# Late weight and input loads tied to 23 score rounds instead of 19, in a two-layer attention and feed-forward kernel

## Chip, core and metric

The kernel runs on one core of a Trainium2 chip. The metric is the device time of one execution in microseconds, the median of several; lower is better. The core's engines are TensorE (PE: matmuls), VectorE (DVE), ScalarE (ACT), GpSimd (POOL) and SyncE (SP), which here issues nearly all DMA transfers.

## What is computed

The input x has 2048 tokens of width 640. Two layers are applied, each an attention block and a feed-forward block with residuals, and both layers use the same weights.

```python
for s in range(N):                                    # 4 segments of 512 tokens, 32 heads of 20
    logits = einsum('bhqd,bhkd->bhqk', qs, ks) * scale + mask
    p = softmax(logits)
    a_dot = einsum('bhqk,bhkd->bhqd', p, vs)
    o = g * (phi(qs) @ M) / (phi(qs) @ z + 1e-6) + (1 - g) * a_dot
    M = M + phi(ks)^T vs ;  z = z + sum(phi(ks))      # memory carried to the next segment
x = x + concat(o) @ wo                                # attention, on layernorm(x)
x = x + relu(layernorm(x) @ w1) @ w2                  # feed-forward, 640 -> 1728 -> 640
# ... both once more
```

Here phi(t) is t + 1 for positive t and exp(t) otherwise; all data are bf16.

## The kernel before

**Work.** One segment of 512 tokens goes through these steps, and several segments are in flight at once. Layer norm on DVE and POOL gives xn_tok, which a DMA transpose turns into xnT (L710). PE projects q and k into stg and v into v_aug (`group`, L667 and L670). The q and k of a segment are spilled to a scratch tensor in HBM (L955) and read back into pad with four heads side by side, two groups of four heads, a "pair", at a time (L1002). Scores are small matmuls from pad (L1186), four at once on quarters of the rows of the array. ACT takes exp of them into PT (L1248), POOL cuts the causal triangle (L1260), PE multiplies by v (L1280), a DMA transpose turns the sums (otu) into otk, and DVE divides (L1366 to L1374). The memory M is read with L1066 and updated with L1123. Then follow wo (L1402 adds the residual), the second layer norm, and the feed-forward block: w1 with relu into hT (L1484, L1485) and hR (L1466), and w2 (L1506 adds the residual).

**Rounds.** A pair has five score rounds (`ROUNDS`), each with two ACT exps; the event ("ex", m, u) says that round u of pair m has been issued, with the tickets of its exps. A segment has four pairs, a layer 16, the kernel 32 and so 160 rounds. Pair 4 is the first of the second segment.

**Order.** All instructions are put in order before the kernel runs, by a planner written into the kernel (`Sched`). Each step of the work is a generator that yields operations with costs and the semaphores that they wait for. In a loop the planner takes the operation that can start first by its own clock, a priority breaking ties, and appends it to its engine's list; what runs on the chip is these fixed lists, each in order, with semaphore waits between them. A DMA load by `dma()` is an operation of SP with an issue time, a rate and a latency in that clock. A matmul group can be issued in two forms: "full", one 128x128 weight tile per matmul (L667), or "cols", the same as four matmuls with 32 weight columns each (L670). The planner takes the form which the array is in, and counts a switch between "full", "cols" and the scores' "rows" form. Because ties and near ties decide, a shift of one operation can reorder what comes after it.

**Loads.** `loads()` fetches the first two segments of x and the weights wq, wk and wv at the start. `late_loads()` fetches the rest through SP's queue, piece by piece, each at first held until a given round has been reached: `n2` is the number of pieces without w2, that is four of x (segment 2), five of wo, four of x (segment 3) and ten of w1 (five with the first half of its columns, name w10, five with the second, w11). The w2 pieces follow from round 25 on, two a round, and wait for a buffer that shares w2's memory (`w2w`); the change leaves them alone. The wait of a piece is on the first exp of its round (`w[:1]`), and SP handles its list in order: a piece that waits holds back the spills, fills and transposes behind it.

Of the kernel before, what the change touches and what calls it, by code (L numbers as in the profile page):

```python
# [38 lines left out]
class Prog:  # L39
# [44 lines left out]
    def dma(self, e, fn, sem):  # L84
        self.pos[e] += 1
        self.dcnt[id(sem)] = self.dcnt.get(id(sem), 0) + 16
        tk = (sem, self.dcnt[id(sem)])
        self.ops[e].append(("op", fn, sem, 16))
        self.info[(id(sem), tk[1])] = ("dma%d" % id(sem), tk[1], dict(self.K[e]))
        return tk  # L90
# [332 lines left out]
def bass_interleave_layers__memory_aug_infini_attn__dense_activation_relu__prompt_kernel(  # L423
    nc, A_x, A_wq, A_wk, A_wv, A_wo, A_beta, B_x, B_w1, B_w2, out,
):
    with contextlib.ExitStack() as es:
# [119 lines left out]
        def late_loads():  # L546

            def x_pieces(s):
                def one(t):
                    return lambda e: e.dma_start(x_sb[:, t, :], xs[:, t, :])  # L550
                return [("x%d" % s, 163840, one(4 * s + i)) for i in range(4)]

            def rows(name, w, src, k):
                return (name, 163840, lambda e: e.dma_start(w[:, k, :], src[128 * k:128 * k + 128, :]))

            def half(k, h):
                cs = slice(h * (DFF // 2), (h + 1) * (DFF // 2))
                return ("w1%d" % h, 221184, lambda e: e.dma_start(w1_r[:, k, cs], B_w1[128 * k:128 * k + 128, cs]))

            pieces = x_pieces(2)  # L560
            pieces += [rows("wo", wo_r, A_wo, k) for k in range(FC)]
            pieces += x_pieces(3)
            pieces += [half(k, h) for h in range(2) for k in range(FC)]
            n2 = len(pieces)
            pieces += [rows("w2", w2_r, B_w2, k) for k in range(NFULL)]
            pieces += [("w2", 81920, lambda e, z=z: e.dma_start(
                w2_r[64 * z:64 * z + DREM, NFULL + z, :], B_w2[NFULL * 128:DFF, :])) for z in range(2)]
            z1 = yield Need("z1")
            sems = {}
            left = {}  # L570
            for name, _, _ in pieces:
                left[name] = left.get(name, 0) + 1
            for n, (name, nbytes, fn) in enumerate(pieces):
                if name not in sems:
                    sems[name] = sem_("d_" + name)
                w = yield Need("ex", *divmod(25 + (n - n2) // 2 if n >= n2 else n * 19 // n2, 5))
                if n == n2:
                    v0 = yield Need("v00")
                    q1 = yield Need("q01")
                    w2w = v0 + q1 + early_done  # L580
                tk = yield dma("sp", sems[name], nbytes, fn, w[:1] + (w2w if n >= n2 else []) + z1, issue=400.0, lat=4500.0)
                left[name] -= 1
                if left[name] == 0:
                    S.set(name, tks=[tk])
# [1009 lines left out]
        S.add(7, consts())  # L1594
        S.add(8, loads())
        S.add(8, late_loads())
        S.run()
        P.waits("sp", [S.last])
# [31 lines left out]
```

The softmax here doesn't subtract the row's maximum and nothing guards it: scores larger than these inputs give would overflow.

## Time and profile before

Time: 556.6 us, the median of 3 runs (555.76 to 557.23). The profiled execution has a span of 554.8 us at a granted TensorE clock of 1.0.

| What | Profile |
|---|---|
| first score round, last score round | 18.5 us, 476 us |
| exps of round 18 and of round 22 end | 58.9 us, 75.6 us |
| SP issues the late pieces of x, wo and w1 | 20.9 to 60.8 us |
| first matmul with w1 | 91.7 us |
| SP issues the w2 pieces | 98.4 to 107.8 us |
| DMA: mean rate, bytes | 110 GB/s, 61.3 MB |

How to read it: the page gives for each engine its busy time and, in the chain, how much of the work that ended last lay on it. A PE row of the timeline merges equal matmuls that follow each other: its start, the time to the end of the last one, its count, and in brackets idle time before it with the instruction that ended it. Matmuls overlap, so the cost of one is the distance from its start to the start of the next, not its length. For a DMA the start is that of its issue, and the landing is given apart.

### The profile page before, as it was taken

How to read it: one execution, taken by the hardware profiler on the slowest of the kernel's cores; microseconds unless marked ns; L12 is line 12 of the kernel's file. 1: busy time of each engine (PE TensorE's matmuls, PEld its weight loads, DVE VectorE, ACT ScalarE, POOL GpSimd, SP SyncE). 2: the span in 40 equal slices, each digit the busy share in tenths (PEclk: the TensorE clock that was granted, in tenths of full speed). 3: DMA queues.
4: the chain of work that ended last, by engine and by line, in shares of the span. 5: the costliest groups of instructions: out<-in, count | busy, mean ns of one | idle time of the engine just before them, and what ended most of it. 6: DMA issues, size and time to landing. Idle time of an engine off the chain costs nothing.

```text
span 554.8 us, 18665 instructions
## 1 busy us (share of the span) xinstructions
PE 545.8 (98%) x8130; PEld 309.3 (56%) x8130; DVE 412.2 (74%) x1061; ACT 407.3 (73%) x516; POOL 190.0 (34%) x302
## 2 busy tenths in 40 slices
PE   8999999999999999999999999999999999999997
PEld 7454554455564555646456544665545654666656
DVE  4967989898799888897878898769885787435102
ACT  5699889889877987798788887679987678432140
POOL 5245344333344344343433443135331443201000
DMA  8595989924945148256176521772439412353101
GB/s 272 131 235 156 222 181 224 231 50 70 187 100 89 39 105 180 50 97 98 21 193 131 92 45 38 184 134 39 69 63 213 95 34 34 84 78 63 40 2 51
DMA packets 130291, 61.30 MB, mean 110 GB/s; under 512 B 109090, under 2 KB 120098, under 8 KB 130210
## 3 DMA queue, kind: packets, MB, share of 16 engines
q1 hardware_dynamic: 129648, 59.58, 50.2%
q8 instruction: 64, 1.05, 0.8%
q10 hardware_dynamic: 562, 0.53, 0.3%
q14 instruction: 17, 0.14, 0.1%
HBM read 20.57 MB, written 12.85 MB: 60 GB/s over the span
## 4 chain that ended last, share of the span: by engine, by line
PE 93%; ACT 2%; DVE 2%; DMA 2%; SPq 0%; issue 0%; POOL 0%; ACTq 0%; POOLq 0%
PE ps L667 45%; PE ps L670 26%; PE ps L1186 9%; PE ps L1280 6%; ACT PT L1248 2%; PE ps L1319 1%; PE ps L1066 1%; PE ps L1123 1%; PE ps L644 1%; DMA otk<-otu 1%; PE ps L1460 1%; DMA beta_bc<-in_A_beta_dram 1%; SPq L982 0%; ACT stg L867 0%; PE ps L758 0%
## 5 line engine op out<-in xcount | busy, mean ns | idle before, releaser
L1248 ACT ACTIVATE PT<-ps 128x1024 bf16<-128x1024 f32 x320 | 308.9, 1027 | 65.0 <-PE ps L1186 59.5
L1260 POOL TENSOR_SCALAR_AFFINE_SELECT PT<-PT 128x512 bf16<-128x512 bf16 x256 | 164.2, 659 | 264.4 <-ACT PT L1248 264.3
L667 PE MATMUL ps<-w_r,hT 128*128 128x320 bf16 x510 | 82.4, 300 | 0.0
L1506 DVE TENSOR_TENSOR x_sb<-x_sb,ps 128x320 bf16<-128x320 bf16 (+1 forms) x65 | 31.1, 478 | 58.9 <-PE ps L670 44.2
L670 PE MATMUL ps<-xnT,w_r 128*32 128x512 bf16 x1112 | 65.4, 379 | 0.2 <-issue 0.2
L1186 PE MATMUL ps<-pad 20*128 20x512 bf16 (+3 forms) x1024 | 63.4, 301 | 1.1 <-ACT PT L1248 0.9
L667 PEld LDWEIGHTS ps<-w_r,hT 128*128 128x128 bf16 x510 | 47.6, 98 | 24.6 <-issue 6.8
L667 PE MATMUL ps<-xnT,w_r 128*128 128x512 bf16 x242 | 59.9, 380 | 0.9 <-DVE hT L1484 0.9
L688 DVE BATCH_NORM_STATS2 stats<-x_sb 128x6 f32<-128x320 bf16 x124 | 55.7, 474 | 2.9 <-DMA x_sb<-in_A_x_dram 2.5
L1485 ACT ACTIVATE hT<-ps 128x512 bf16<-128x512 f32 x56 | 33.4, 597 | 22.9 <-PE ps L670 20.7
L670 PE MATMUL ps<-w_r,hT 128*32 128x320 bf16 (+1 forms) x1340 | 49.0, 294 | 0.0
L1186 PEld LDWEIGHTS ps<-pad 20*128 20x128 bf16 x1024 | 17.9, 92 | 52.1 <-ACT PT L1248 27.8
L1402 DVE TENSOR_TENSOR x_sb<-x_sb,ps 128x320 bf16<-128x320 bf16 x64 | 30.0, 479 | 18.2 <-PE ps L667 10.3
L670 PEld LDWEIGHTS ps<-xnT,w_r 128*32 128x32 bf16 x1112 | 29.0, 97 | 25.2 <-issue 0.4
L1280 PE MATMUL ps<-PT,v_aug 128*21 128x128 bf16 (+3 forms) x896 | 40.4, 301 | 0.0
L670 PEld LDWEIGHTS ps<-w_r,hT 128*32 128x32 bf16 x1340 | 34.8, 97 | 9.0
L667 PE MATMUL ps<-wo_r,oT 128*128 128x320 bf16 x242 | 38.9, 300 | 0.0
L1290 DVE CAST otu<-ps 128x512 bf16<-128x512 f32 x48 | 32.7, 682 | 6.9 <-PE ps L1280 6.3
L1484 DVE TENSOR_SCALAR hT<-ps 128x512 bf16<-128x512 f32 x48 | 32.7, 681 | 6.5 <-PE ps L667 4.3
L704 POOL TENSOR_TENSOR rstd<-lnU,mhalf 128x2 f32<-128x2 f32 (+2 forms) x26 | 20.6, 791 | 46.1 <-DVE lnU L700 43.1
L667 PEld LDWEIGHTS ps<-xnT,w_r 128*128 128x128 bf16 x242 | 21.6, 98 | 25.6 <-issue 4.6
L866 DVE CAST stg<-ps 128x512 bf16<-128x512 f32 x45 | 30.6, 684 | 5.8 <-PE ps L667 5.6
(109 smaller groups left out, 736.9 us busy)
## 6 DMA issues: line engine op xcount, KB each, us to landing
pad<-scr SPq DMA_DIRECT2D x124, 80.0 KB
scr<-stg SPq DMA_DIRECT2D x34, 256.0 KB, 3.1
out_dram<-x_sb SPq DMA_DIRECT2D x15, 160.0 KB, 1.8
w_r<-in_B_w_dram SPq DMA_DIRECT2D x10, 216.0 KB, 2.6
w_r<-in_B_w_dram SPq DMA_DIRECT2D x13, 160.0 KB, 2.9
x_sb<-in_A_x_dram SPq DMA_DIRECT2D x10, 160.0 KB, 3.2
scr<-w_r SPq DMA_DIRECT2D x5, 256.0 KB, 3.2
wv_r<-in_A_wv_dram SPq DMA_DIRECT2D x1, 800.0 KB, 8.8
```

What stands on the lines that cost most here:

```text
L667: return e.matmul(view(dst.ap, b), a, b, start=(k == 0), stop=(k == last))
L670: return e.matmul(view(dst.ap[rows], b), part, b, start=(k == 0), stop=(k == last))
L688: tk = yield dve(320, 1, lambda e, c2=c2: e.bn_stats(stats6[:, t % 12, c2, :], x_sb[:, t, c2 * 320:(c2 + 1) * 320]), xt)
L866: te = yield evac(N, 1, lambda e: e.tensor_copy(sg.ap[:, t0:t0 + N], bk.ap[:, 0:N]), lambda e: e.activation(sg.ap[:, t0:t0 + N], bk.ap[:, ...
L1186: fns.append([(lambda e, z=z, j=j, hh=hh, N=N, o=o, sl=sl, q=hh % 2: e.matmul(slot.ap[:, q, o:o + N], sl.ap[32 * hh:32 * hh + DH, z, 0, 12 ...
L1248: tx = yield act(1024, lambda e, dst=dst, src=src: e.activation(dst, src, ACT.Exp, scale=SCALE), sc + pw)
L1260: tm = yield pool(600.0, lambda e, reg=reg: e.affine_select(out=reg, in_=reg, pattern=[[0, 4], [1, 128]], compare_op=ALU.is_ge, fill=0.0, ...
L1280: fns.append((lambda e, OD, j=j, hh=hh: e.matmul(OD.ap[32 * hh:32 * hh + DH + 1, 128 * j:L], VAUG[vx(a, s)][:, j, 4 * g + hh, :], pt.ap[:, ...
L1290: te = yield evac(L, 1, lambda e: e.tensor_copy(dst, OD.ap), lambda e: e.activation(dst, OD.ap, ACT.Copy), [tk] + OTU[0].tks)
L1484: th = yield evac(512, 1, lambda e: e.tensor_scalar(hT[:, dc, :], bk.ap[:, :], 0.0, None, ALU.max), lambda e: e.activation(hT[:, dc, :], b ...
L1485: lambda e: e.activation(hT[:, dc, :], bk.ap[:, :], ACT.Relu), [tk] + HT.tks)
L1506: ta = yield dve(n, 1, lambda e: e.tensor_tensor(x_sb[:, t, c0:c0 + n], x_sb[:, t, c0:c0 + n], bk.ap[:, 0:n], ALU.add), [tk], urgent=True)
```

## The change

One number in `late_loads()`: the pieces before w2 are spread over 23 rounds instead of 19. As there are 23 such pieces, piece n is now held until round n, where before some rounds took two pieces. It is meant to thin out the late loads, so that SP's queue and the DMA engines have room in between for the spills, fills and transposes of the first segments. The loads themselves, their sizes and their order among each other stay the same.

```diff
-                w = yield Need("ex", *divmod(25 + (n - n2) // 2 if n >= n2 else n * 19 // n2, 5))
+                w = yield Need("ex", *divmod(25 + (n - n2) // 2 if n >= n2 else n * 23 // n2, 5))
```

## Prediction

> **What bounds the kernel now.** I read the page's busy shares and chain first.
>
> ```profile
> PE 545.8 (98%) x8130; PEld 309.3 (56%) x8130; DVE 412.2 (74%) x1061; ACT 407.3 (73%) x516; POOL 190.0 (34%) x302
> PE 93%; ACT 2%; DVE 2%; DMA 2%; SPq 0%; issue 0%; POOL 0%; ACTq 0%; POOLq 0%
> ```
>
> TensorE carries 93% of the chain that ends last. Busy PE is not proof, since matmuls overlap in the trace, so I looked at start-to-start times in the PE timeline.
>
> ```profile
> 361.07 1.52 PE L667 MATMUL ps<-w_r,hT 128*128 128x320 bf16 x10
> 362.52 0.40 PE L1186 MATMUL ps<-pad 20*128 20x256 bf16 x8
> 362.85 0.58 PE L667 MATMUL ps<-w_r,hT 128*128 128x320 bf16 x3
> 540.04 1.94 PE L670 MATMUL ps<-w_r,hT 128*32 128x320 bf16 x52
> 541.81 0.31 PE L670 MATMUL ps<-w_r,hR 128*32 128x320 bf16 x4
> ```
>
> A full 128x320 matmul is 0.1355 us apart from the next. In column form four matmuls do the same work: 52 in 1.77 us is 0.136 us per four. So the two forms cost the same. The ten in the first row would need 1.36 us and the score row comes after 1.45 us; the eight score matmuls need 0.23 us and the next row comes after 0.33 us. Going into score form and out of it thus costs some 0.1 us each way, 0.21 us a round. Adding such start-to-start prices (full: 0.2155 us for 512 columns, 0.1355 for 320, 0.0665 for 147 and so on; an L1186 round 0.22 to 0.23) over all matmuls between 18.5 us and the last one at 551.5 us gives 524.4 us of the 533 us elapsed. Only some 9 us are waits; the rest is work in order. The table by stage shows where the waits are.
>
> ```profile
> 67.60:81.30 13.70, 13.70 (x165) 7.58 (x164) 11.77 (x31) 11.52 (x15) 4.38 (x8) 1.00 0.85 187
> 81.30:95.00 13.70, 13.36 (x222) 5.83 (x218) 13.20 (x33) 12.83 (x17) 6.72 (x10) 1.00 1.07 218
> 95.00:109.70 14.70, 13.84 (x161) 6.30 (x157) 11.67 (x34) 12.36 (x16) 6.09 (x10) 1.00 0.98 234
> 109.70:124.30 14.60, 14.60 (x187) 7.60 (x186) 13.46 (x32) 12.82 (x16) 4.46 (x8) 1.00 0.23 59
> ```
>
> After length come busy time of PE, PEld, DVE, ACT and POOL, clock, DMA share and GB/s. The two stages from 81.3 to 109.7 us have the DMA engines full and PE short of work. By my prices PE needed 12.9 and 13.6 us there, so 0.8 and 1.1 us were lost. Later stages lose about 0.1 us each. The largest single loss is this:
>
> ```profile
> 98.36 1.31 SPq L554 DMA_DIRECT2D w_r<-in_B_w_dram  x3
> 99.72 1.24 SPq L710 DMA_TRANSPOSE otk<-otu  x1
> 101.00 6.15 SPq L554 DMA_DIRECT2D w_r<-in_B_w_dram  x10
> ```
>
> (the DMA issues of SP), then VectorE and PE in the same stretch:
>
> ```profile
> 105.29 0.35 DVE L1366 RECIPROCAL rden<-otk 128x32 f32<-128x32 bf16 x1 [1.03 <-DMA otk<-otu]
> 106.65 0.68 DVE L1484 TENSOR_SCALAR hT<-ps 128x512 bf16<-128x512 f32 x1
> ```
>
> ```profile
> 107.39 2.33 PE L667 MATMUL ps<-xnT,w_r 128*128 128x512 bf16 x10 [0.86 <-DVE hT L1484]
> ```
>
> Three w2 loads stand ahead of the transpose that fills otk. It lands 5.6 us after issue (median of all otk transposes 3.2 us), VectorE sits 1.03 us at L1366, the eviction behind it is late, and PE waits for the bank.
>
> **What the Trainium skill says.** "TensorEngine Tiling (Array Packing)", Key Properties: changing the tiling mode drains TensorE. The trace agrees, 0.1 us a change. "DMA: Bandwidth & Descriptors", Anatomy of one DMA — SWDGE (gpsimd) path: DMA engines do not wait on semaphores, the issuing sequencer does before dispatch. So a load waiting for its round holds back everything behind it in SP's queue; in the SP waits L558 waits 9.6 us for ACT in total, longest 1.5 us. Same page, Queues, rings and completion order: each engine takes descriptors in ring order; the late otk above fits.
>
> **The change part by part.** There are 23 pieces (4 x, 5 wo, 4 x, 10 w1), so piece n now waits for round n instead of 19n/23. It removes no transfer and no instruction of the function itself; it moves times, and the planner then orders everything anew.
>
> 1. Loads of x and wo. The last x piece of segment 2 goes from round 2 to round 3, those of segment 3 from rounds 7 to 9 to rounds 9 to 12. In the trace round 12 ends at 47.8 us; segment 3 is normalised after 70 us, and wo is first used at 71.0 us. Cost zero, hidden by the attention of the first segment.
>
> 2. Loads of w1. The first half ends with round 17 instead of 14, the second with round 22 instead of 18, that is by 75 us. Its first use is at 91.7 us. But in the changed SP order the last three pieces (216 KB each) stand behind two xnT transposes and a spill, so they are issued near 84 us instead of 54 to 61 us: into the stage whose DMA share is already 1.07. Three issues at 0.48 us make 1.45 us; SP waits 0.8 us at that point anyway (the phk transpose behind it starts at 84.88, the spill before it ended at 84.05), so the phk, otk and xnT transposes behind them start 0.6 us later. PE needs that xnT at 92 us: it was issued at 88.14 and lands 3.5 to 4.0 us later, 91.6 to 92.1; PE already lost 0.33 us at L670 at 91.73. Moved by 0.6 us less the score round that the new order puts first (0.33 us), plus slower landing by the extra 0.66 MB (0 to 1 us; 0.66 MB at 218 GB/s would be 3 us, most of it over before the xnT is issued): loss +0.3 us at least, +1.3 us at most; I take +0.6.
>
> 3. w2 against otk. In the new order the second otk transpose stands ahead of all w2 loads, after eight pad fills as before. Then it should land in 3.2 to 4 us, not 5.6: VectorE's 1.03 us shrinks to 0 to 0.5 us, and PE's stall, 1.03 us start to start, by 0.5 to 1.0, in the middle 0.75. But VectorE has 10.9 us of work in the four rounds around it, by the durations of its rows, against 10.8 us of PE work, so some of it may come back. I take -0.75.
>
> 4. PE work. Up to 91.7 us the PE and, up to 90 us, the VectorE order are the same in both programs. After it the new order has 58 fewer full matmuls of L667 and 232 more of L670, four for one: 70 of 320 columns went to column form, 12 of 512 to full form, each at equal price within 0.001 us. The memory update L1123 runs less often in column form, where it skips heads: 12 full matmuls more (0.82 us), 48 narrow ones fewer (0.45 us), +0.37. Score rounds between full groups go from 75 to 69, those with a column group on one side from 84 to 89, on both sides 1 to 2; with one more direct change full to column that is +0.15 us. In sum +0.5 us, and it is on the path.
>
> 5. Later order. From the first score of a pair to that of the next PE has some 13.8 us of work; from pair 23 to 24 it was 24.1 us and from 27 to 28 23.8, because the scores wait for their pads; now it is 34.9 and 15.4. In all of them PE has filler. The new pair 28 has the tightest fill: its last eviction, spill issue, four fill issues and landing must fit in 7.3 us of PE work. Eviction 0.9, spill issue 0.35, fills 4 x 0.34 = 1.4, landing: not given for pad, bounded by 3.7 us after the last issue at 63.8 us (score at 67.6 us). Sum at most 6.4 us, so it fits. By way of the second spill it is 11.1 us of PE work against 0.9 + an otk issue of 1.4 + 0.35 + 3.1 (spill landing, page part 6) + 1.4 + 3.7 = 10.9 us, just so. Other waits on landings (xn, oT, phk) have within 0.4 us the same least distance as before. I take 0, with 1.5 us at the far end. The last 1308 matmuls are the same.
>
> Sum: +0.6 - 0.75 + 0.5 + 0 = +0.35 us on the median of 556.6: **556.9 us**.
>
> **The rivals.**
> - Faster, 554.4 us: both waits from 81 to 110 us go, not one. For it: 1.9 us are lost there, and one half has a cause that the new order takes away. Add a third of the 2.3 us of small losses from 124 to 465 us (341 us against 338.5 us of priced work), 0.8 us, for a luckier order; less 0.5 us more work: -2.2 us. Against it: in the stage from 81 us ACT now has 11.8 us of work against PE's 11.8, and the DMA is fuller.
> - Slower, 559.0 us: the w1 loads in the full DMA stage delay xnT by more than 1 us (+1.3), otk is late as before, so nothing is gained (0), work +0.5, and one late fill at pair 28 (+0.6): +2.4 us. For it: DMA share 1.07; the planner puts the load into a stage where the chip is fuller than it assumes. Against it: fewer w1 loads around 50 us do nothing for PE, but the waits that the trace shows are seldom on DMA: of PE's waits only L670's 0.2 us could be.
>
> **How the numbers follow.** The main case, two small effects that cancel, has 0.55 and reaches from 554.9 to 558.3; faster 0.19; slower 0.26, the larger because the work grows and the new waits are of more kinds than those removed. 0.3% is 1.7 us, so the cases are the three classes. For 8 in 10: 554.6 to 559.0.
>
> **What would show it.** PE start to start before L1460 near 92 us (part 2), the landing of the second otk transpose and VectorE's gap at L1366 near 104 us (part 3), the time from the first w1 use to the last matmul against 0.5 us more (part 4), no gap at pairs 24 and 28 (part 5). A PE gap of over 1 us anywhere after 125 us would make the prediction wrong, and so would early stages, up to 81 us, of another length, since their PE order is unchanged.

## The result and the profile after

The changed kernel takes 560.4 us (559.68 to 561.64), the kernel before, run beside it, 556.4 us (555.76 to 557.23). The ratio is 1.0074, 95% interval [1.0051, 1.0097]: some 4 us slower, above the range of the prediction (554.6 to 559.0). The traced execution of the changed kernel is its fastest (559.68 us), so the traces below show 2.9 us of the 4.

The page of the changed kernel, busy shares and chain:

```profile
span 557.7 us, 18907 instructions
PE 545.8 (98%) x8250; PEld 307.7 (55%) x8250; DVE 420.2 (75%) x1069; ACT 403.5 (72%) x508; POOL 192.8 (35%) x302
...
PE 85%; DVE 6%; DMA 4%; ACT 3%; SPq 1%; issue 1%; POOL 0%
```

TensorE's busy time is the same 545.8 us, and the span is 2.9 us longer. In the chain 8% moved from PE to DVE, DMA, ACT and SP's queue: at more places PE was released by something else. That is no measure of lost time, as 8% of the span would be 45 us. The table by stage (length, busy time of PE, PEld, DVE, ACT and POOL, clock, DMA share, GB/s), with the same windows as before:

```profile
67.60:81.30 13.70, 13.70 (x165) 7.58 (x164) 11.83 (x31) 11.53 (x15) 4.45 (x8) 1.00 1.03 196
81.30:95.00 13.70, 12.77 (x200) 5.63 (x201) 12.81 (x30) 12.59 (x17) 7.12 (x11) 1.00 1.15 237
95.00:109.70 14.70, 14.16 (x149) 6.18 (x151) 12.11 (x37) 12.02 (x15) 5.69 (x9) 1.00 0.97 245
109.70:124.30 14.60, 14.60 (x181) 7.33 (x174) 13.76 (x33) 13.18 (x17) 5.38 (x9) 1.00 0.37 76
```

The w1 loads fill the second stage still more (share 1.15 for 1.07), and PE is busy 0.6 us less in it. From 95 us on PE is not worse off by this table. The waits behind that are in the PE timeline, the last three of them outside the table; the brackets give the idle time and what ended it:

```profile
91.70 0.40 PE L1186 MATMUL ps<-pad 20*128 20x384 bf16 x8 [0.19 <-ACT PT L1248]
92.66 0.73 PE L1460 MATMUL ps<-xnT,w_r 128*32 128x256 bf16 x20 [0.56 <-issue]
105.41 0.82 PE L667 MATMUL ps<-xnT,w_r 128*128 128x512 bf16 x3 [0.41 <-DVE hT L1484]
142.59 0.85 PE L667 MATMUL ps<-wo_r,oT 128*128 128x320 bf16 x5 [0.79 <-DMA oT<-o_sb]
264.14 0.40 PE L1186 MATMUL ps<-pad 20*128 20x512 bf16 x4 [0.65 <-ACT PT L1248]
369.32 0.40 PE L1186 MATMUL ps<-pad 20*128 20x512 bf16 x4 [0.29 <-DMA pad<-scr]
```

The same view of the kernel before has, after 91 us, the wait at 91.73, the one at 107.39 and 0.18 us at 330 us. Taken start to start, as in the prediction (distance to the next matmul, less the usual distance of such a pair), the waits are:

| Place in the changed kernel | What is waited for | before, us | after, us |
|---|---|---|---|
| 92 us | xnT for the first w1 rows, exp | 0.33 | 0.89 |
| 105 to 108 us | evictions behind otk | 1.03 | 1.03 |
| 142 us | oT transpose | 0 | 0.96 |
| 250 us | VectorE's otu | 0 | 0.31 |
| 264 us | exp of the round before | 0 | 0.72 |
| 367 to 369 us | oT, then the pad of pair 24 | 0 | 0.61 |
| sum | | 1.36 | 4.52 |

Up to the score round at 91.7 us the two executions are equal (91.73 and 91.70 us). The sum grows by 3.2 us, a little more than the 2.9 us of the span; small waits, the 0.5 us of work that the prediction expected and the difference of one execution from the next are not separated here. 2.6 of the 3.2 us lie after 140 us, long after the last load that was moved.

### The profile page after: what moved, and what is told of

It is laid out like the page before. It is cut to its first block, busy times and chain, and to the rows that moved or that the text cites. A ratio compares the mean times of both kernels' runs of the same rounds, so it can differ in the third digit from the quotient of the medians.

```text
span 557.7 us, 18907 instructions
## 1 busy us (share of the span) xinstructions
PE 545.8 (98%) x8250; PEld 307.7 (55%) x8250; DVE 420.2 (75%) x1069; ACT 403.5 (72%) x508; POOL 192.8 (35%) x302
## 4 chain that ended last, share of the span: by engine, by line
PE 85%; DVE 6%; DMA 4%; ACT 3%; SPq 1%; issue 1%; POOL 0%
PE ps L667 41%; PE ps L670 25%; PE ps L1186 8%; PE ps L1280 6%; ACT PT L1248 2%; PE ps L1066 1%; DMA pad<-scr 1%; PE ps L1123 1%; PE ps L1319 1%; DMA oT<-o_sb 1%; PE ps L1460 1%; DMA otk<-otu 1%; DVE o_sb L1374 1%; DVE stats L688 1%; DMA beta_bc<-in_A_beta_dram 1%
## 5 line engine op out<-in xcount | busy, mean ns | idle before, releaser
L1260 POOL TENSOR_SCALAR_AFFINE_SELECT PT<-PT 128x512 bf16<-128x512 bf16 x256 | 167.2, 671 | 244.7 <-ACT PT L1248 244.6
L667 PE MATMUL ps<-w_r,hT 128*128 128x320 bf16 x477 | 77.4, 300 | 0.0
L667 PE MATMUL ps<-xnT,w_r 128*128 128x512 bf16 x262 | 64.1, 380 | 0.5 <-DVE hT L1484 0.4
L670 PE MATMUL ps<-xnT,w_r 128*32 128x512 bf16 x1032 | 61.4, 379 | 0.0
L667 PEld LDWEIGHTS ps<-w_r,hT 128*128 128x128 bf16 x477 | 43.9, 98 | 22.6 <-issue 6.1
L670 PE MATMUL ps<-w_r,hT 128*32 128x320 bf16 (+1 forms) x1472 | 54.2, 294 | 0.0
L670 PEld LDWEIGHTS ps<-w_r,hT 128*32 128x32 bf16 x1472 | 38.4, 97 | 10.0
L1290 DVE CAST otu<-ps 128x512 bf16<-128x512 f32 x52 | 35.5, 684 | 10.6 <-PE ps L1280 10.5
L1031 ACT ACTIVATE stg<-stg 128x512 bf16<-128x512 bf16 x50 | 31.6, 635 | 6.9 <-DVE rtmp L1029 6.7
L667 PE MATMUL ps<-wo_r,oT 128*128 128x320 bf16 x213 | 33.6, 300 | 0.8 <-DMA oT<-o_sb 0.8
```

The source lines that it names most:

```text
L667: return e.matmul(view(dst.ap, b), a, b, start=(k == 0), stop=(k == last))
L670: return e.matmul(view(dst.ap[rows], b), part, b, start=(k == 0), stop=(k == last))
L1031: te = yield act(512, lambda e, q=q: e.activation(q, q, ACT.Exp), [tr] + p, psum=False)
L1260: tm = yield pool(600.0, lambda e, reg=reg: e.affine_select(out=reg, in_=reg, pattern=[[0, 4], [1, 128]], compare_op=ALU.is_ge, fill=0.0, ...
L1290: te = yield evac(L, 1, lambda e: e.tensor_copy(dst, OD.ap), lambda e: e.activation(dst, OD.ap, ACT.Copy), [tk] + OTU[0].tks)
```

## The experiments

The change does two things at once: it moves loads in SP's queue, and the planner, seeing other times, puts the work of all engines from 91.7 us on into another order. Theory **order**: the new order costs the time. Theory **loads**: the later loads do. A third theory, **fetch**, came from the list of DMA packets in the trace. Besides the data there are packets of kind "instruction". Those of 16 KB come one per 128 matmuls in the median of the kernel before, which makes 64 bytes for each matmul and each weight load. The Trainium skill, "Runtime: NRT & Kernel Launch", Instruction fetch mechanics, says what they are: an engine's program is refilled in 16 KiB blocks of 256 instructions over a DMA queue of its own, and the cost of that is "mostly hidden". The sizes and counts agree. By this theory the cost is not hidden from the transfers beside it. In the changed kernel one of them falls on the oT transpose that PE waits for at 142.6 us:

```
                                  issued           instruction packets near, us (ns)      landing after issue
before, oT transposes             137.6, 139.0     138.17 (8 KB, 512), 144.55 (1271)      3.8, 3.8 us
after, oT transposes              136.8, 138.1     139.22 (931), 139.62 (8 KB, 1698)      5.4 to 5.8 us
before, second otk transpose      99.72            101.63 (1352)                          5.6 us
after, second otk transpose       99.30            95.56 (955)                            4.8 us
```

No load was in flight at 139 us. The median 256-byte packet takes 18 ns; in the changed kernel 44 data packets took over 400 ns, up to 1507, half of them starting from 139.4 to 139.7 us, the others at 141.4 us. The short 8 KB packet at 138.17 us in the kernel before did no harm.

### Loads and order apart: two mirror kernels

The planner's decisions are recorded and its lists are written out again with only SP's loads of x, wo and w1 at other places, with the waits for the other rounds. All other lists stay as they are, instruction by instruction. (`LOAD_AT` says behind how many other SP transfers each load stands.)

```diff
-        P.waits("sp", [S.last])
+        Q = Prog(P.clk); replay(S, Q, LOAD_AT); Q.waits("sp", [S.last])
...
-            P.emit(block)
+            Q.emit(block)
...
+LOAD_AT = [14, 14, 16, 23, 23, 29, 29, 29, 29, 29, 33, 33, 33, 33, 33, 33, 33, 33, 33, 33, 33, 35, 38]
```

That is the changed order with the loads as before. The mirror has the order before with the changed kernel's places (..., 35, 38, 38, 63, 63, 63).

> The order of the changed kernel on TensorE, VectorE, ScalarE and GpSimd, instruction by instruction; only SyncE's loads of x, wo and w1 stand where they stood before the change and wait for the rounds of the spread over 19. Theory order (the planner's new order from 91.7 us on costs the time, by landings that TensorE now waits for at 142.6, 264.1 and 367.5 us; when the loads come is nothing): 559.5 to 560.5 us, with the waits at 142, 264 and 367 us still there; at most 0.6 us comes back near 92 us, where the first row of w1 waits. Theory loads (216 KB pieces of w1 in the full DMA stage near 84 us cost the time directly): 556.5 to 557.5 us, and the waits after 125 us are gone too.

> The mirror of the run before: the order of the kernel before on all engines but SyncE, whose loads of x, wo and w1 stand where the change puts them and wait for the rounds of the spread over 23. Theory order: 556.4 to 557.0 us, no wait of TensorE over 0.5 us after 125 us, 0.3 to 0.6 us more near 92 us. Theory loads: 559.5 us or more.

| | loads as before (19) | loads as changed (23) |
|---|---|---|
| order before | 1 | 1.0025 [1.0009, 1.0041] |
| order changed | 1.0055 [1.0038, 1.0073] | 1.0074 [1.0051, 1.0097] |

Neither theory's times came true: with early loads 558.5 us, with late loads in the order before 557.5 us, each between the two ranges that were expected. The order by itself costs 0.55%, some 3 us; its interval is clear of 1. So is that of the late loads in the order before, 0.25%, 1.4 us. In the changed order the loads make 0.19%, 1.1 us, but there the two intervals overlap, so this part is not resolved. The prediction took 0.6 us for the loads.

In the order before, the late loads act where the prediction looked. PE's first w1 row that reads the xnT, in the kernel before and with the late loads:

```profile
91.73 0.61 PE L670 MATMUL ps<-xnT,w_r 128*32 128x512 bf16 x8 [0.16 <-issue]
```

```profile
93.41 0.61 PE L670 MATMUL ps<-xnT,w_r 128*32 128x512 bf16 x8 [0.95 <-issue]
```

Start to start the wait grew from 0.33 to 1.12 us; no wait over 0.5 us comes after 125 us, as the order theory expected. Another 0.9 us between these two executions arose before 38 us, where pairs of executions with equal orders differ by steps of 0.5 to 1 us anyway.

In the changed order, two kernels with equal lists can be compared matmul by matmul. Against the changed kernel the early loads gain 0.63 us at 92 us (and lose 0.36 again at once), 1.05 us at 104 to 108 us, and 0.16 us at 142 us, where the wait on oT stays, as do those at 264 and 367 us, which the loads theory expected to go:

```profile
91.89 0.40 PE L1186 MATMUL ps<-pad 20*128 20x384 bf16 x8 [0.19 <-ACT PT L1248]
94.32 0.39 PE L1186 MATMUL ps<-pad 20*128 20x512 bf16 x4 [0.29 <-ACT PT L1248]
141.35 0.85 PE L667 MATMUL ps<-wo_r,oT 128*128 128x320 bf16 x5 [0.63 <-DMA oT<-o_sb]
```

(PE timeline of the changed order with early loads.) How three late w1 loads reach as far as 105 us is seen in SP's issues. First the changed kernel, then the same order with early loads:

```profile
83.44 1.47 SPq L558 DMA_DIRECT2D w_r<-in_B_w_dram  x3
84.95 1.23 SPq L710 DMA_TRANSPOSE phk<-phs  x1
86.23 2.81 SPq L710 DMA_TRANSPOSE otk<-otu  x1
89.08 1.41 SPq L710 DMA_TRANSPOSE xnT<-xn_tok  x1
...
94.00 4.87 SPq L1002 DMA_DIRECT2D pad<-scr  x8
98.91 0.34 SPq L955 DMA_DIRECT2D scr<-stg  x1
99.30 1.30 SPq L710 DMA_TRANSPOSE otk<-otu  x1
```

```profile
85.01 1.24 SPq L710 DMA_TRANSPOSE phk<-phs  x1
86.33 2.05 SPq L710 DMA_TRANSPOSE otk<-otu  x1
88.42 1.44 SPq L710 DMA_TRANSPOSE xnT<-xn_tok  x1
...
93.37 3.94 SPq L1002 DMA_DIRECT2D pad<-scr  x8
97.35 0.35 SPq L955 DMA_DIRECT2D scr<-stg  x1
98.94 1.25 SPq L710 DMA_TRANSPOSE otk<-otu  x1
```

With the loads in between, SP needs 2.81 instead of 2.05 us to issue one otk transpose, comes to the xnT 0.66 us later, and needs 4.87 instead of 3.94 us for eight fills. The second otk, issued 0.36 us later, lands after 4.8 instead of 3.7 us, and VectorE and then PE wait for it. This is read from one execution of each.

### One part of the change alone, and its neighbours

x and wo keep the spread over 19, only w1 gets that over 23:

```diff
-... else n * 23 // n2, 5))
+... else (n * 19 // n2 if n < 13 else n * 23 // n2), 5))
```

> One part of the change alone: x and wo by the spread over 19, only the ten w1 loads by the spread over 23. The planner makes the changed kernel's order of it on TensorE, VectorE, ScalarE and GpSimd, so all of the loss is expected: 559.5 to 560.5 us, ratio 1.006 to 1.009, with the waits at 92, 105, 142, 264 and 367 us of the changed kernel. If the x and wo loads had a part in it: under 559 us.

559.3 us, ratio 1.0062 [1.0044, 1.0079], the ratio as expected and the time 0.2 us below its range. All the engines but SP have the changed kernel's lists. So w1 alone brings the new order and the loss; x and wo have no part that can be measured.

Then 21 and 22 rounds in place of 23:

> The loads spread over 21 rounds. The planner makes the order of the kernel before on TensorE, VectorE, ScalarE and GpSimd of it, and of the w1 loads one, not three, stands in the stage near 84 us. Order theory with a part for the loads in proportion (e2: three of them cost 0.25%): 0.08% slower than before, 556.2 to 556.8 us against 556.2, so no change that can be measured. If a spread over more rounds is bad in itself: half of the 0.74%, some 558 us.

> The loads spread over 22 rounds, one less than the change. The planner makes another order of it, unlike both kernels, in whose own plan TensorE sits idle 3.6 us after 90 us (2.8 us in the changed kernel's, 1.4 us in that of before). Order theory: 560 to 562 us, slower than with 23 although the loads come earlier, with the plan's waits in the trace (near 107 us on VectorE, near 115 us on w2). Loads theory: between 21 and 23, at most 559.5 us.

With 21 the lists are those of before, one w1 load stands near 84 us, and the time is the same: 555.8 us, 0.9998 [0.9981, 1.0016]. With 22 the planner makes yet another order, and the time jumps to 558.1 us, 1.0042 [1.0029, 1.0054]. The order theory had expected 560 to 562 us, slower than with 23, because the plan has more idle time in it than the changed kernel's. That missed. The time lies where the loads theory put it, between 21 and 23 and below 559.5 us: near 84 us stand no w1 load with 19 rounds, one with 21, two with 22 and three with 23. This run changes order and loads together and cannot tell them apart; only the two mirror kernels do.

### Moving the instruction packets

The 52 warm-up matmuls at the start, ahead of all work, are cut into 104 of half the width, or merged into 13 of four times the width. No other instruction changes, but each 16 KB packet falls 52 matmuls earlier or 39 later against the work.

```diff
-                ps[:, 0, 0:128], ident[:], ident[:], start=True, stop=True), k == 51) for k in range(52)], idt)
+                ps[:, 0, 0:64], ident[:], ident[:, 0:64], start=True, stop=True), k == 103) for k in range(104)], idt)
```

> The changed kernel with its 52 warm-up matmuls of 128 columns, ahead of all work, cut into 104 of 64 columns; all else is the same instruction by instruction. TensorE's instructions come by DMA in packets of 16 KB, one for about 128 matmuls, so each such packet now falls 52 matmuls earlier against the work. Theory fetch (which of the transposes and fills land late is decided by the instruction packet that crosses them): the waits at 142.6, 264.1 and 367.5 us change, at least two of the three by over 0.4 us, others appear, and the time moves by 1 us or more from 560.4 us, either way. Rival (the waits belong to the order alone): the same three waits with the same lengths within 0.2 us, time within 0.6 us of 560.4.

> The changed kernel with its 52 warm-up matmuls of 128 columns made into 13 of 512 columns, so that the instruction packets fall 39 matmuls later against the work; all else is the same. Theory fetch: the waits at 142.6, 264.1 and 367.5 us change and the time moves by 1 us or more from 560.4 us, either way, and not to the same value as with 52 more. Rival (order alone): the same three waits, time within 0.6 us of 560.4.

In both kernels the wait at 142.6 us is gone, 0.96 us less start to start. This is the same spot with 104 matmuls; the row with wo_r follows its forerunner without a wait:

```profile
142.15 0.60 PE L667 MATMUL ps<-xnT,wq_r 128*128 128x512 bf16 x2
142.59 0.84 PE L667 MATMUL ps<-wo_r,oT 128*128 128x320 bf16 x5
```

and the answers on the tile oT, from 100 to 150 us, first of the changed kernel, then with 104 matmuls:

```profile
L710 SPq DMA_TRANSPOSE oT<-o_sb x2: 1327/1392/1458, 136.8 to 138.1; - x2
...
DMA to landing us min/median/max: 5.4/5.6/5.8
```

```profile
L710 SPq DMA_TRANSPOSE oT<-o_sb x2: 1327/1388/1449, 137.7 to 139.1; - x2
...
DMA to landing us min/median/max: 3.9/4.1/4.3
```

The instruction packets now come at 131.92 and 144.01 us, none between issue and landing but a short one at 140.63 us (8 KB, 309 ns). With 13 matmuls one at 141.03 us (1549 ns) falls late on both transposes, issued at 137.45 and 138.81 us, and they take 4.3 and 5.4 us. The early-loads kernel, in which the packet still crosses (137.98 us, transposes issued from 135.68), kept 5.2 to 5.6 us. But the times moved by less than the 1 us expected: 559.4 us (1.0072 [1.0053, 1.0091]) and 560.0 us (1.0091 [1.0066, 1.0115]), neither clear of the changed kernel's 1.0074. The waits at 264 and 367 us stayed, which misses the expectation of two of three. At 105 to 108 us PE lost 1.05 and 0.9 us less, but near 92 us PE lost 0.9 and 1.1 us more, and with 104 matmuls 0.87 us at a pad at 68.6 us. So where the packets fall decides single landings; the sum did not measurably change.

The same edit on the kernel before:

> The kernel before with its 52 warm-up matmuls cut into 104 of half the width; every other instruction of every engine is the same. In the kernel before a 16 KB instruction packet at 101.63 us (1352 ns) crosses the second otk transpose, issued at 99.72 and landed 5.6 us later. With 52 more matmuls that packet falls some 3 us earlier, between 97 and 99 us. Theory fetch: that otk lands 3.2 to 4.2 us after its issue, VectorE's 1.03 us at L1366 shrinks to under 0.4 us, TensorE's wait near 107.4 us (1.03 us) to under 0.4 us; time 555.0 to 555.6 us against 556.0 if no other wait appears. Rival (the w2 loads ahead of it in the queue make it late, as the prediction said): landing 5 us or more and the wait at 107.4 us as before; time within 0.5 us of before.

The second otk (issued at 103.69 us, the packet ahead of it at 101.85 us) lands after 3.4 us, though the three w2 loads stand ahead of it as before; the wait at 107 us is gone (1.03 us less). With the same three loads ahead and a packet across it, it took 5.6 us before, 5.9 with late loads, 4.9 with 21 rounds, and 5.3, 5.8 and 4.5 in the three versions below. VectorE goes on without idle time:

```profile
106.76 0.49 DVE L1081 TENSOR_TENSOR om_sb<-ps,rmem 128x320 bf16<-128x320 f32 x1
107.17 0.34 DVE L1366 RECIPROCAL rden<-otk 128x32 f32<-128x32 bf16 x1
```

The time is that of before all the same: 555.9 us, 1.0001 [0.999, 1.0013]. In the traced execution, PE's wait near 92 us has grown in its place. Another packet, at 82.62 us (2812 ns), now falls on two xnT transposes, which hold SP for 5.26 us, where they held it for 3.25; the xnT behind them, which PE waits for, is issued 1.37 us later and lands after 5.1 instead of 3.5 us, itself with a packet across it (92.51 us). SP before, SP with 104 matmuls, then PE:

```profile
80.07 3.25 SPq L710 DMA_TRANSPOSE xnT<-xn_tok  x2
...
88.14 1.44 SPq L710 DMA_TRANSPOSE xnT<-xn_tok  x1
```

```profile
80.86 5.26 SPq L710 DMA_TRANSPOSE xnT<-xn_tok  x2
...
89.51 1.45 SPq L710 DMA_TRANSPOSE xnT<-xn_tok  x1
```

```profile
94.71 0.61 PE L670 MATMUL ps<-xnT,w_r 128*32 128x512 bf16 x8 [2.21 <-issue]
```

This execution is the slowest of its 22 (558.4 us, the median is 555.9), so a wait of this length is not the usual one.

Both remedies on the changed order at once:

> The run with the changed order and the early loads, with 104 warm-up matmuls instead of 52. If the waits named so far add up: the early loads take away the waits at 92 and 105 us, the shifted packet the one at 142 us (0.63 us there, up to 0.97 start to start); left are those at 250, 264 and 367 to 369 us, 1.6 us in sum, and 0.5 us more matmul work, less the 1.03 us that only the kernel before waits at 107 us. So 556.6 to 557.4 us against 556.0 of before and 558.5 without the shift. If the packets decide nothing: 558.5 as without the shift.

557.7 us, 1.0031 [1.0012, 1.005], against 1.0055 with the early loads alone. In the trace 0.81 us go at the oT wait and no other step over 0.3 us comes after 38 us. So in the trace the waits do add up. The time does not settle it: it is 0.3 us above the expected range and 0.8 us below the 558.5 us of the rival, and its interval holds both. By the same sum what is left, 0.3%, would be the waits at 250, 264 and 367 to 369 us and the extra work.

### The two waits that stay

At 264 us no transfer is late. ScalarE's lines of the changed kernel:

```profile
259.35 1.94 ACT L1248 ACTIVATE PT<-ps 128x1024 bf16<-128x1024 f32 x2 [0.81 <-PE ps L1186]
261.19 0.44 ACT L921 ACTIVATE v_aug<-ps 128x320 bf16<-128x320 f32 x1
262.06 1.94 ACT L1248 ACTIVATE PT<-ps 128x1024 bf16<-128x1024 f32 x2 [0.43 <-PE ps L1186]
```

A round's two exps take 1.94 us and start 0.43 us after the scores, and the next round's scores, which wait for them, start 2.5 us after the last; from 261.63 to 264.14 us the order has only 1.8 us of matmuls, the scores included, and PE waits for the difference. The planner's own clock has a gap of 0.89 us there too. At 367 to 369 us oT and the pad of pair 24 come late; their transfers stand one behind the other in SP's queue:

```profile
359.76 3.18 SPq L710 DMA_TRANSPOSE xnT<-xn_tok  x2
362.98 2.16 SPq L710 DMA_TRANSPOSE oT<-o_sb  x1
365.19 6.03 SPq L1002 DMA_DIRECT2D pad<-scr  x15
```

In the w1-alone kernel, with the same lists and traced in its slowest execution, this pad wait was 1.66 us in place of 0.29, so its size is not fixed by the order. No run takes these two waits away by themselves; that they make up the rest is read from the trace, not shown by an edit.

### Other orders

Three versions were meant to beat both kernels. Only weights of the planner's choices and the rounds of the loads are changed, for the first:

```diff
-LONE_NS = 300.0
+LONE_NS = 250.0
-SOFT = 400
-SOFT_DMA = 1000
+SOFT = 450
+SOFT_DMA = 850
...
-... divmod(25 + (n - n2) // 2 if n >= n2 ...
+... divmod(23 + (n - n2) // 2 if n >= n2 ...
```

> A version meant to beat both kernels: the loads spread over 19 as before, the planner's weights for its own choices changed (LONE_NS 250 for 300, SOFT 450 for 400, SOFT_DMA 850 for 1000, w2 from round 23 on instead of 25), so that it makes a third order in whose plan TensorE sits idle 0.6 us after 90 us, against 1.4 us in the plan of the kernel before and 2.8 us in that of the changed one. If what the plan of an order already shows as idle decides: 555 to 556 us, the same or 0.2% faster than before. If the landings that a plan does not know decide: 557 to 560 us, with waits of TensorE on transposes or fills that no plan shows.

> A second version meant to beat both: spread over 19, and a planner that counts a landing as 1.5 us less sure instead of 1.0 (SOFT_DMA 1500), SOFT 450, LONE_NS 350; idle in its plan after 90 us 1.15 us. If slack ahead of landings pays: no wait of TensorE on a transpose or fill after 110 us, 554.5 to 555.7 us against 556.2 of before. If not: 556 to 558 us.

> A third version meant to beat both: spread over 22, SOFT 350, SOFT_DMA 1150, LONE_NS 350, COLS_LAG 1800, w2 from round 24; its plan ends earliest of all (0.5 us before that of the kernel before), with idle near 91.5 and 99 us. If the plan decides: 555.5 to 556.2 us although the loads come later. If late loads or unplanned landings decide: 557 to 559 us.

| Order | PE idle in the plan after 90 us | w1 loads near 84 us | ratio to before |
|---|---|---|---|
| before | 1.4 us | 0 | 1 |
| changed | 2.8 us | 3 | 1.0074 [1.0051, 1.0097] |
| changed, early loads | 2.8 us (planned with 23 rounds) | 0 | 1.0055 [1.0038, 1.0073] |
| 22 rounds | 3.6 us | 2 | 1.0042 [1.0029, 1.0054] |
| first of the three | 0.6 us | 0 | 0.9998 [0.998, 1.0016] |
| second (SOFT_DMA 1500) | 1.15 us | 0 | 0.9988 [0.9975, 1.0001] |
| third (22 rounds, plan that ends earliest) | 1.75 us | 2 | 1.0026 [1.0013, 1.0039] |

None beats the kernel before by more than its interval; the second, which plans more slack before landings, comes nearest (555.6 us), and its expectation, no wait on a transpose or fill after 110 us, is met. What is left in it is the pair of waits at 92 and 108 us that the kernel before has, the first of them longer:

```profile
92.60 0.62 PE L670 MATMUL ps<-xnT,w_r 128*32 128x512 bf16 x8 [0.93 <-issue]
108.27 2.33 PE L667 MATMUL ps<-xnT,w_r 128*128 128x512 bf16 x10 [0.86 <-DVE hT L1484]
```

An instruction packet crosses its otk, too (103.42 us; otk issued at 100.59). The trace is of its slowest execution, 557.0 us. The first version, 556.4 us, lies between its two expected ranges. The third's plan ends earliest and it is slower, 557.8 us, as expected if late loads or unplanned landings decide.

The plan's idle time splits the orders: at most 1.4 us in those that are not slower than before, 1.75 us or more in those that are. It does not give the size, as 22 rounds, with the most idle time, lose less than 23. But among the kernels run as planned, the number of late w1 loads splits them in the same way, and three such loads cost 0.25% in the order before, without any change of order. For 22 rounds and the third version it is therefore open whether order or loads cost the time; only the changed order was run without its late loads.

## Why the prediction was wrong

- **Part 1 (x and wo cost nothing)** held: w1 alone brings the same order and the same loss.
- **Part 2 (w1 near 84 us: +0.6 us, at most +1.3)** had the right mechanism, and the runs give its term 1.1 to 1.4 us, the first of these not clear of noise. The part at 92 us was 0.56 us in the changed kernel, as predicted (0.79 us for late loads in the order before); missed was that SP's slower issues go on through the fills to the second otk and, in the traced pair, its waits at 105 us. I followed the delay to the first consumer that waits and stopped there.
- **Part 3 (the second otk ahead of w2: -0.75 us)** failed in its cause. It said that three w2 loads made the otk late. In the kernel before with shifted instruction packets the same three loads stand ahead of it and it lands after 3.4 us, not 5.6; in the changed kernel none stands ahead and it took 4.8 us. VectorE's gap fell only from 1.03 to 0.87 us, and PE's loss there stayed at 1.03 us. The gain was nil. With early loads the same order had it: otk landed after 3.7 us and PE did not wait there. So in this pair of traces the loads of part 2 took back the gain of part 3, and the prediction had added the two as if they were apart. The loads alone do not fix it: with 104 matmuls they stand at the same places and this otk landed after 3.1 us. No instruction packet crosses the otk of the changed kernel, so what slowed it to 4.8 us stays open.
- **Part 4 (+0.5 us of work)** was not tested by itself. The waits of the table already make up the longer span, so the traces leave room for it only if small waits shrank; it stays open.
- **Part 5 ("I take 0, with 1.5 us at the far end")** is the step that failed most: 2.6 us after 125 us. It compared the least distances of the new order with one landing time of each transfer, as if that were fixed, and asked only for late transfers. The fill that I named as the tightest, pair 28's, cost nothing. The oT transpose, 3.8 us in the trace of before, needed 5.4 to 5.8; the pad of pair 24, which I gave 34.9 us of work, waited behind other transfers in SP's queue; and the largest but one, at 264 us, was no landing, but ScalarE's pace of 2.5 us a round. The planner's own clock, which the prediction did not read, had 1.4 us more idle time in the new order before anything ran. The sign that was to prove the prediction wrong, a gap over 1 us after 125 us, did not come in this trace: there were several below 1 us. That these waits make the order's loss is read from the trace; the edits show that the order costs some 3 us, not which wait does. Early stages of equal length, its other sign, held.
- The slower rival was right in kind (xnT late, otk late as before, 0.5 us of work, a late landing) and too small: it allowed one late landing after 125 us.

In short: by the medians the load change itself costs a quarter to a third of the loss, the new order the rest. Whether most other orders that this planner can make are worse than that of before is not shown: of the three that ran with early loads, one is slower (0.55%) and two are not.

## What to carry to other kernels

Where a planner orders the work, price a change to its inputs in two parts: the change with the order held fixed, and the new order. The second can be the larger, and writing out the old lists with the change put in tells them apart. Read the planner's idle time for the new order before the run: here it grew from 1.4 to 2.8 us. Take a transfer's landing as a spread, not as its median, and follow a delayed queue through all transfers behind it, not only to the first wait.

## What the runs showed of the hardware that was not expected

TensorE's program comes by DMA during the run, and it is not free for the data: 64 and 65 packets of 16 KB in the two kernels, 0.9 to 2.8 us each in the runs looked at, and transfers that one crosses tend to land late. In the traces of all 14 kernels, after 110 us, oT transposes in whose first 3 us such a packet starts landed after 4.7 us (median of 53), the others after 3.6 us (136); for otk it is 4.1 us (132) against 3.1 us (232). The ranges overlap, oT from 3.35 to 5.8 us with a packet and to 5.7 us without, so a packet is not the only cause, nor does each one delay. In the kernel before, of 344 packets of up to 2 KB that took over 700 ns, 280 started within 1.5 us of an instruction packet's start (16 or 8 KB); those stretches are 41% of the time. Merging or cutting 52 matmuls at the start moved these packets, and waits of 1 us a hundred microseconds later went and came; the time of the kernel did not change by more than its noise. Why they slow their neighbours, the trace does not tell. The Trainium skill, "DMA: Bandwidth & Descriptors", Queues, rings and completion order, offers one way: the increment of a transfer's semaphore lands only after every earlier write from that DMA engine, across its queues, so one large packet on one of 16 engines could hold back the landing of a whole transfer. The late landings fit this, but no run separates it from other ways. How long a crossed transfer takes also differs from run to run: with 21 rounds, at the same places, the otk took 4.9 us and PE did not wait.
